# Attention and two MLPs on one core: eight steps' values scaled after the value matmul by sums from the tensor engine, with eight start-up banks, spread weight conversions and moved transfers

## The chip, the cores and the metric

One core of a Trainium2 chip runs the whole program in one launch. The metric is device time in microseconds (us), taken as the median of the runs. The profile is one execution of the same program, recorded by the hardware profiler. Five engines matter: TensorE (PE; weight loads are a row of their own, PEld), VectorE (DVE), ScalarE (ACT), GpSimd (POOL) and SyncE (SP), which issues most transfers.

## The reference

The inputs are 4 batches of 8 heads: 512 local and 32 global tokens of 64 features each. Local queries see the keys within 32 positions and all global keys; global queries see everything.

```python
def sm(s):
    s = s - np.max(s, axis=-1, keepdims=True)
    e = np.exp(s)
    return e / (np.sum(e, axis=-1, keepdims=True) + 1e-09)
...
s_l = np.concatenate([s_lg, s_ll], axis=-1)     # local rows: 32 global keys, then the masked local ones
a_l = sm(s_l)
out_l = np.matmul(a_l, np.concatenate([v_g, v_l], axis=2))
...
x = np.ascontiguousarray(attn_out.transpose(0, 2, 1, 3)).reshape(B * S, H * D)   # 2176 x 512
h = x @ w_in                       # first MLP, 512 -> 2048 -> 512
g = np.maximum(0.01 * h, h)
y = g @ w_out
h2 = y @ w2_in                     # second MLP, the same sizes
out = (h2 - np.tanh(h2)) @ w2_out
```

## The kernel before

**The attention.** The work on local queries is cut into 32 steps `pp`: two heads and a half (256 rows) of a batch each. `stage(s)` emits one slot of a software pipeline: transposes of keys and queries of step s+1 (`k_prep`, `q_prep`), scores of step s (`score`, tile `sps`), their softmax (`smax_a`, `smax_b`), the value matmuls of step s-2 (`av`, tile `avps`), scores of the global queries (`g_score`, `sgps`) and the transposes of the probabilities of step s-1 (`p_trans`, `ptps`). Every few stages a global query block is worked off (`g_smax`, `g_trans`, `g_av`).

In `smax_a` VectorE takes the minimum of the negated scores and ScalarE the exponential, with the row sum as a second output (`accum_out`). `smax_b` forms the reciprocal of four row sums per partition. For steps 0 to 7 GpSimd then multiplies the exponentials `e` by it (L453, two instructions of 128x512); for later steps VectorE does (L458). `p_trans` transposes the normalised `e` on TensorE and copies it out (`pt`; for steps 0 to 7 the second head's copy is VectorE's, L472). `av` multiplies by the values, and ScalarE (L500) and VectorE (L502) split the result into a high and a low part, `xh` and `xl`.

**The MLPs.** Every product is made of three float32r matmuls (high by high, low by high, high by low), so `mlp1_a` and `mlp1_b` issue 12 matmuls each per item. An item n is one 128-wide slice `f` of the hidden layer for one chunk `c` of tokens. Items 0 to 7 run beside stages 10 to 17, items 24 to 31 beside stages 18 to 21, items 32 to 63 beside the rest; items 8 to 23 have no attention beside them. The hidden tile `h` has one PSUM bank, so the next item's first matmul waits until ScalarE has read it (L206).

**Weights.** They come as 64-bit floats, two 32-bit words each. `convert_w` makes a 32-bit float of them with one ScalarE instruction (L128) and three of VectorE (L129, L133, L136); `split_w` makes the high and low parts (L142, L143). Four slices of `w_in` are converted in the start-up (stages 0 to 9), the others beside the items. `job()` converts slices of the other three matrices; each needs a raw tile `wraw`, of which there are two, fetched by SyncE in order. The table `job_at` says how many jobs an item has; the entry `early` adds one to some items.

**What sets the order.** TensorE runs in the order of the program text up to item 78. The other engines' order is set by a scheduler from the text's priorities and `issue_after`, which names an instruction that another must follow on its queue. Each engine runs its own list strictly in order. In the start-up seven PSUM banks are handed out in turn (`start_tags`), later three.

## Time and profile before

| what | value |
|---|---|
| median of 3 runs | 928.71 us (926.78 to 930.80) |
| the profiled execution | 928.65 us |
| its span, first to last instruction | 926.9 us |
| PE busy | 903.5 us (97%) |
| DVE busy | 628.0 us (68%) |
| ACT busy | 538.4 us (58%) |
| POOL busy | 38.8 us (4%) |
| mean granted TensorE clock | 0.998 of full speed |

The shares of the whole span say little here, because TensorE is busy nearly everywhere. What is open to a change is read from the stretches in which TensorE waits or runs small matmuls: the start-up (0 to about 64 us), and single waits later. Busy time of an engine in a stretch, the chain of waits through it and the single instructions on either side of a wait are the views to read.

### The profile page before, as it was taken

How to read it: one execution, taken by the hardware profiler on the slowest of the kernel's cores; microseconds unless marked ns; L12 is line 12 of the kernel's file. 1: busy time of each engine (PE TensorE's matmuls, PEld its weight loads, DVE VectorE, ACT ScalarE, POOL GpSimd, SP SyncE). 2: the span in 40 equal slices, each digit the busy share in tenths (PEclk: the TensorE clock that was granted, in tenths of full speed). 3: DMA queues.
4: the chain of work that ended last, by engine and by line, in shares of the span. 5: the costliest groups of instructions: out<-in, count | busy, mean ns of one | idle time of the engine just before them, and what ended most of it. 6: DMA issues, size and time to landing. Idle time of an engine off the chain costs nothing.

```text
span 926.9 us, 15545 instructions
## 1 busy us (share of the span) xinstructions
PE 903.5 (97%) x5468; PEld 766.3 (83%) x5468; DVE 628.0 (68%) x1373; ACT 538.4 (58%) x1245; POOL 38.8 (4%) x73
## 2 busy tenths in 40 slices
PE   7889999999899999999999999999999999999998
PEld 5667778887688999888889998888888888899897
DVE  3877867856545655643232459878888888888886
ACT  5888875444556666643233457555656655655664
POOL 4510000000000000000000000000000000000022
PEclk9999999999999999999999999999999999999999
DMA  8777798678866887767556662001000100010010
GB/s 191 189 195 196 220 282 265 199 220 273 278 187 180 246 227 235 221 211 226 174 187 199 222 199 92 1 1 59 22 1 24 46 1 0 1 47 1 1 35 24
DMA packets 146830, 129.22 MB, mean 139 GB/s; under 512 B 89536, under 2 KB 108992, under 8 KB 146752
## 3 DMA queue, kind: packets, MB, share of 16 engines
q1 hardware_dynamic: 144096, 127.57, 45.9%
q8 instruction: 43, 0.70, 0.3%
q10 hardware_dynamic: 2656, 0.66, 0.3%
q14 instruction: 35, 0.29, 0.1%
HBM read 101.45 MB, written 26.74 MB: 138 GB/s over the span
## 4 chain that ended last, share of the span: by engine, by line
PE 81%; DMA 6%; DVE 5%; ACT 5%; issue 1%; POOL 1%; SPq 0%; ACTq 0%; POOLq 0%; DVEq 0%
PE h L55 35%; PE o L55 20%; PE y L55 16%; DMA wf<-w2od 4%; PE sps L55 3%; PE ptps L469 2%; DMA wraw<-in_moe_w_out_dram 2%; ACT e L439 1%; PE avps L55 1%; DVE e L432 1%; PE gavps L55 1%; PE sgps L55 1%; PE kps L368 1%; ACT g L206 1%; DVE wf L136 1%
## 5 line engine op out<-in xcount | busy, mean ns | idle before, releaser
L55 PE MATMUL h<-xh,win 128*128 128x512 f32 (+2 forms) x1280 | 355.5, 361 | 1.6 <-ACT g L206 1.6
L55 PEld LDWEIGHTS h<-xh,win 128*128 128x128 f32 x1280 | 229.2, 188 | 34.3 <-ACT g L206 2.8
L55 PE MATMUL h<-xl,win 128*128 128x512 f32 (+2 forms) x640 | 229.0, 358 | 0.0
L55 PEld LDWEIGHTS h<-xl,win 128*128 128x128 f32 x640 | 120.5, 188 | 15.3
L55 PE MATMUL y<-gh,woh 128*128 128x512 f32 (+2 forms) x320 | 119.6, 374 | 0.0
L55 PE MATMUL y<-gh,wol 128*128 128x512 f32 (+2 forms) x320 | 114.9, 359 | 0.0
L55 PE MATMUL y<-gl,woh 128*128 128x512 f32 (+2 forms) x320 | 113.9, 359 | 0.0
L208 DVE TENSOR_TENSOR gl<-g,gh 128x512 fp32r<-128x512 f32 (+2 forms) x80 | 48.8, 611 | 90.4 <-ACT gh L207 86.3
L55 PE MATMUL o<-wo2l,gh 128*128 128x512 f32 x255 | 99.6, 391 | 0.0
L55 PE MATMUL o<-wo2h,gh 128*128 128x512 f32 x255 | 99.4, 390 | 0.0
L55 PE MATMUL o<-wo2h,gl 128*128 128x512 f32 x255 | 97.7, 390 | 0.0
L657 ACT ACTIVATE u<-h 128x512 f32<-128x512 f32 (+2 forms) x80 | 42.6, 533 | 93.1 <-PE h L55 86.2
L206 ACT ACTIVATE g<-h 128x512 f32<-128x512 f32 (+2 forms) x80 | 42.4, 530 | 73.4 <-PE h L55 73.2
L682 ACT ACTIVATE gh<-p 128x512 fp32r<-128x512 f32 (+2 forms) x80 | 45.5, 568 | 41.0 <-DVE p L666 41.0
L55 PEld LDWEIGHTS y<-gl,woh 128*128 128x128 f32 x320 | 60.5, 189 | 8.0
L55 PEld LDWEIGHTS y<-gh,woh 128*128 128x128 f32 x320 | 60.5, 189 | 7.6 <-issue 0.2
L55 PEld LDWEIGHTS y<-gh,wol 128*128 128x128 f32 x320 | 60.7, 190 | 6.5
L439 ACT ACTIVATE e<-e,st 128x224 f32<-128x224 f32 (+1 forms) x88 | 40.4, 460 | 29.1 <-DVE st L432 28.9
L663 ACT ACTIVATE u<-u,consts 128x512 f32<-128x512 f32 (+2 forms) x80 | 52.7, 659 | 6.9 <-DVE p L661 4.1
L683 DVE TENSOR_TENSOR gl<-p,gh 128x512 fp32r<-128x512 f32 (+1 forms) x64 | 41.9, 654 | 21.9 <-ACT gh L682 21.8
L55 PEld LDWEIGHTS o<-wo2h,gl 128*128 128x128 f32 x255 | 47.9, 188 | 10.2
L55 PEld LDWEIGHTS o<-wo2h,gh 128*128 128x128 f32 x255 | 48.0, 188 | 9.0
(111 smaller groups left out, 1401.1 us busy)
## 6 DMA issues: line engine op xcount, KB each, us to landing
wraw<-in_moe_w_out_dram SPq DMA_DIRECT2D x32, 512.0 KB, 4.6
woh<-wod SPq DMA_DIRECT2D x64, 256.0 KB, 3.9
wol<-wod SPq DMA_DIRECT2D x64, 256.0 KB, 3.4
inraw<-in_moe_w_in_dram SPq DMA_DIRECT2D x16, 512.0 KB, 5.9
wraw<-in_moe_w_in_dram SPq DMA_DIRECT2D x16, 512.0 KB, 5.3
vr<-in_v_l_dram SPq DMA_DIRECT2D x48, 96.0 KB, 3.8
kr<-in_k_l_dram SPq DMA_DIRECT2D x47, 96.0 KB, 3.2
wod<-woh SPq DMA_DIRECT2D x16, 256.0 KB, 4.2
```

The source lines that it names most:

```text
L55: nc.tensor.matmul(o, lhsT, rhs, start=start, stop=stop)
L136: nc.vector.scalar_tensor_tensor(out=w.bitcast(I32), in0=lw, scalar=29, in1=t, op0=ALU.logical_shift_right, op1=ALU.bitwise_or)
L206: nc.scalar.activation(g[:, :N], h[:, :N], AF.Prelu, alpha=0.01)
L208: anchor[0] = nc.vector.tensor_sub(gl[:, :N], g[:, :N], f32(gh)[:, :N])
L368: nc.tensor.transpose(ps[:, c : c + n], kr[:n, t].rearrange("p h d -> p (h d)"), ident[:n, :n])
L432: nc.vector.tensor_tensor_reduce(out=e[:, h, j, s0 : s0 + n], in0=ps[h][:, j * 256 : j * 256 + n], in1=mask[:, a, j, :n], op0=ALU.add, op1 ...
L439: last_exp[0] = nc.scalar.activation(e[:, h, j, s0 : s0 + n], x, AF.Exp, bias=st[:, k : k + 1], scale=-1.0, accum_out=st[:, 4 + k : 5 + k],)
L469: nc.tensor.transpose(ps[:, at : at + n], e[:n, h, j, c0 : c0 + 128], ident[:n, :n])
L657: nc.scalar.activation(u, h, AF.Square)
L663: nc.scalar.activation(u, u, AF.Square, bias=tc_a2)
L682: nc.scalar.activation(gh[:, :N], p, AF.Copy)
L683: eng["pool" if i == order2[-1] else "dve"].tensor_sub(gl[:, :N], p, f32(gh)[:, :N])
```

## The change

Steps 0 to 7 (`late`) no longer normalise `e`. The exponential has no second output, and `smax_b` does nothing for them. In `av`, besides the eight matmuls by the values, eight more multiply the same transposed `e` by a constant block of ones (`ones`, 64 columns of `consts`), so that the other half of the same bank holds each query's row sum, repeated over the 64 rows of its head. VectorE adds 1e-9 (L510), takes the reciprocal of 128x256 (L511) and multiplies (L512); the copy and the difference that split the result read that product.

The start-up hands out eight banks: `h` joins the seven. The four conversions of the start-up are cut in parts (`convert_parts`) that are emitted between the operations of stages 3, 5, 7 and 9 in place of whole ones after stages 2, 4, 6 and 8. The second jobs of items 22 and 23 go: `early` has 8 entries, 17 among them, and not 9; the later jobs come every 9.5 and not every 9.8 units. The two loads of partial sums in `y_part` must follow the newest fetch of output weights on SyncE's list. In the last chunk of the first MLP, `w2_place` runs behind the newest instructions of the item.

```diff
+    ones = consts[:, 32:96]
...
-    def norm(pp):
-        return "pool" if pp < 8 else "dve"
+    def late(pp):
+        return pp < 8
...
-                    accum_out=st[:, 4 + k : 5 + k],
+                    **({} if late(pp) else {"accum_out": st[:, 4 + k : 5 + k]}),
...
+        if late(pp):
+            return
         nc.vector.tensor_scalar_add(st[:, 4:8], st[:, 4:8], 1.0e-9)
         nc.vector.reciprocal(st[:, 8:12], st[:, 4:8])
-        if norm(pp) == "pool":
-            r = st[:, 8:12].rearrange("p (h j) -> p h j", h=2)
-            for h in range(2):
-                nc.gpsimd.tensor_mul(e[:, h], e[:, h], r[:, h].unsqueeze(2).to_broadcast([128, 2, 256]))
-            return
...
         for j in range(2):
-            for c, (_, n, t, lo, hi) in enumerate(chunks[pp // NP % 2][j]):
-                for h in range(2):
-                    r = slice(64 * h, 64 * h + 64)
-                    q = slice(j * 128 + lo, j * 128 + hi)
+            for k in range(2 if late(pp) else 1):
+                for c, (_, n, t, lo, hi) in enumerate(chunks[pp // NP % 2][j]):
                     at = pt_at[2 * j + c][0]
-                    mm(ps[r, q], v[:n, t, h], pt[h][:n, at + lo : at + hi], c == 0, c == 1)
-        nc.scalar.activation(dh, ps[:, :HALF], AF.Copy)
+                    for h in range(2):
+                        r = slice(64 * h, 64 * h + 64)
+                        q = slice(k * HALF + j * 128 + lo, k * HALF + j * 128 + hi)
+                        mm(ps[r, q], ones[:n] if k else v[:n, t, h], pt[h][:n, at + lo : at + hi], c == 0, c == 1)
+        x = ps[:, :HALF]
+        if late(pp):
+            x = mlp.tile([128, HALF], F32, tag="gl", name="xs", bufs=3)
+            nc.vector.tensor_scalar_add(x, ps[:, HALF:], 1.0e-9)
+            nc.vector.reciprocal(x, x)
+            nc.vector.tensor_mul(x, ps[:, :HALF], x)
+        nc.scalar.activation(dh, x, AF.Copy)
         av_n.append(pp)
-        last_av[0] = nc.vector.tensor_sub(dl, ps[:, :HALF], f32(dh))
+        last_av[0] = nc.vector.tensor_sub(dl, x, f32(dh))
...
-        nc.sync.dma_start(out=f32(x)[:, :, 256:512], in_=yp_dram[:, :, 256 * k : 256 * k + 256])
+        with tc.issue_after(last_fetch[0].ins):
+            nc.sync.dma_start(out=f32(x)[:, :, 256:512], in_=yp_dram[:, :, 256 * k : 256 * k + 256])
...
-    start_tags = ["att0", "att1", "att2", "y0", "y1", "y2", "y3"]
+    start_tags = ["att0", "att1", "att2", "y0", "y1", "y2", "y3", "h"]
...
-        early = n in (11, 12, 13, 15, 16, 18, 20, 22, 23)
+        early = n in (11, 12, 13, 15, 16, 17, 18, 20)
...
-        job_at[n] = int(out_f) + int(early) + int(due / 9.8)
-        due %= 9.8
+        job_at[n] = int(out_f) + int(early) + int(due / 9.5)
+        due %= 9.5
...
-            for op in stage(pp):
+            parts = in_parts() if pp >= 3 and pp % 2 else []
+            for k, op in enumerate(stage(pp)):
                 op()
+                if parts and k != 1:
+                    behind(parts.pop(0))
...
-            if pp >= 2 and pp % 2 == 0:
-                in_job()
...
-                    w2_place(kind, f, t)
+                    behind(lambda: w2_place(kind, f, t))
```

On TensorE, the value matmuls of one start-up step (`vr` are values, `consts` the ones), as a piece of the difference:

```order
 L55 MATMUL avps<-pt,vr 64x128 x2
 L55 MATMUL avps<-pt,vr 64x64 x2
+L55 MATMUL avps<-pt,consts 64x128 x2
+L55 MATMUL avps<-pt,consts 64x64 x2
 L55 MATMUL avps<-pt,vr 64x128 x2
 L55 MATMUL avps<-pt,vr 64x96 x2
+L55 MATMUL avps<-pt,consts 64x128 x2
+L55 MATMUL avps<-pt,consts 64x96 x2
```

Eight matmuls by the ones have come between the eight by the values; the profile counts each of them as two.

On VectorE, stage 4 of the start-up before: `sps_514` are the scores of step 4, `avps_530` the product of step 2, `st` the row sums, `inraw1` a raw slice of `w_in`:

```order
L502 TENSOR_TENSOR xl512_69<-avps_530,xh512_67 128x256
L472 COPY pt_562<-ptps_557 128x480
L448 TENSOR_SCALAR st_523<-st_523 128x4
L129 TENSOR_SCALAR wt_564<-wf_565 128x512
L449 RECIPROCAL st_523<-st_523 128x4
L133 SCALAR_TENSOR_TENSOR wt_564<-inraw1_339,wt_564 128x512
L136 SCALAR_TENSOR_TENSOR wf_565<-inraw1_339,wt_564 128x512
L426 TENSOR_REDUCE st_593<-sps_584 128x2
```

The same stage after the change, where `avps_539` is the product of step 2 and `xs_556` the scaled one:

```order
L136 SCALAR_TENSOR_TENSOR wt_430<-inraw0_217,wt_430 128x512
L510 TENSOR_SCALAR xs_556<-avps_539 128x256
L141 SCALAR_TENSOR_TENSOR wf_418<-inraw0_217,wt_430 128x512
L511 RECIPROCAL xs_556<-xs_556 128x256
L478 COPY pt_579<-ptps_574 128x480
L149 TENSOR_TENSOR win0_498<-wf_418,win0_498 128x512
L512 TENSOR_TENSOR xs_556<-avps_539,xs_556 128x256
L435 TENSOR_REDUCE st_605<-sps_596 128x2
L435 TENSOR_REDUCE st_605<-sps_597 128x2
L515 TENSOR_TENSOR xl512_69<-xs_556,xh512_67 128x256
```

The add and the reciprocal come ahead of the copy of the transposed exponentials, and the minimum of the next step stands behind the product that needs the reciprocal. The conversion of the slice is spread between them.

On ScalarE, from the activation of item 22 on, before (`wf` and `w2f` are conversions that need a `wraw`; `kt` and `qt` belong to stage 18, beside item 24):

```order
L206 ACTIVATE g_2857<-h_2844 128x512
L207 ACTIVATE gh_2858<-g_2857 128x512
L128 ACTIVATE wf_2879<-wraw_2834 128x512
L142 ACTIVATE woh_2884<-wf_2879 128x512
L128 ACTIVATE w2f_2890<-wraw_2842 128x512
L206 ACTIVATE g_2915<-h_2902 128x512
L207 ACTIVATE gh_2916<-g_2915 128x512
L128 ACTIVATE wf_2937<-wraw_2888 128x512
L370 ACTIVATE kt_2963<-kps_2959 128x352
L381 ACTIVATE qt_2968<-qps_2965 128x256
```

The same place after the change:

```order
L212 ACTIVATE g_2923<-h_2910 128x512
L213 ACTIVATE gh_2924<-g_2923 128x512
L129 ACTIVATE wf_2943<-wraw_2863 128x512
L148 ACTIVATE woh_2949<-wf_2943 128x512
L212 ACTIVATE g_2972<-h_2959 128x512
L213 ACTIVATE gh_2973<-g_2972 128x512
L129 ACTIVATE wf_2992<-wraw_2908 128x512
L148 ACTIVATE woh_2998<-wf_2992 128x512
L377 ACTIVATE kt_3019<-kps_3015 128x352
L388 ACTIVATE qt_3024<-qps_3021 128x256
```

Before, three conversions stand between the activation of item 22 and the keys and queries of stage 18, two of them ahead of the activation of item 23; after, there are two, one for each item.

## Rows read from the trace of the kernel before

**Rows 1.** Page, busy per engine, and TensorE's slices of 23 us in tenths:

```profile
PE 903.5 (97%) x5468; PEld 766.3 (83%) x5468; DVE 628.0 (68%) x1373; ACT 538.4 (58%) x1245; POOL 38.8 (4%) x73
...
PE   7889999999899999999999999999999999999998
```

**Rows 2.** Busy time by stretch: start-up stages 2 to 9, then ten-microsecond windows:

```profile
core 0: us, PE busy (x) PEld busy (x) DVE busy (x) ACT busy (x) POOL busy (x), PEclk, DMA share, GB/s
17.22:63.94 46.72, 40.89 (x442) 31.05 (x440) 36.01 (x88) 38.01 (x130) 17.17 (x18) 1.00 0.76 188
...
220.00:230.00 10.00, 9.32 (x42) 7.35 (x41) 6.98 (x12) 4.07 (x7) 0.00 (x0) 1.00 0.85 274
230.00:240.00 10.00, 7.15 (x50) 5.44 (x48) 5.77 (x19) 5.65 (x17) 0.00 (x0) 0.85 1.02 350
...
530.00:540.00 10.00, 9.67 (x55) 9.13 (x53) 3.88 (x6) 4.93 (x10) 0.00 (x0) 1.00 0.75 239
540.00:550.00 10.00, 9.53 (x55) 9.53 (x56) 4.92 (x8) 5.36 (x11) 0.00 (x0) 1.00 0.78 255
```

**Rows 3.** Chain of waits, start-up: start, length, what:

```profile
17.22 1.33 PE sps L55 x10
...
27.52 1.49 PE sps L55 x10
...
45.38 0.87 PE avps L55 x16
...
63.94 0.95 PE sps L55 x8
```

**Rows 4.** Single instructions: start, length, idle before and releaser; stages 1, 2 and 5:

```profile
15.06 0.63 PE L469 MATMUL ptps<-ident,e 128*128 128x128 f32 x4 [0.46 <-POOL e L453]
...
16.06 0.64 PE L469 MATMUL ptps<-ident,e 128*128 128x128 f32 x4 [0.36 <-POOL e L453]
...
16.53 0.47 PE L368 MATMUL kps<-ident,kr 128*128 128x128 f32 x3
...
31.88 0.54 PE L55 MATMUL sps<-mask,ident_b 128*128 128x448 bf16 x2
```

**Rows 5.** Groups by line in stages 2 to 9: count, busy, mean, idle before:

```profile
L136 DVE SCALAR_TENSOR_TENSOR wf<-inraw,wt 128x512 int32<-128x512 int32 x5 | 5.6, 1122 | 0.1
...
L449 DVE RECIPROCAL st<-st 128x4 f32<-128x4 f32 x9 | 1.6, 175 | 0.2
...
L448 DVE TENSOR_SCALAR st<-st 128x4 f32<-128x4 f32 x9 | 1.5, 163 | 0.9 <-ACT e L439 0.8
...
L439 ACT ACTIVATION_READ_ACCUMULATOR e<-sps,st 128x1 f32 x32 | 6.6, 205 | 0.0
```

**Rows 6.** One line's instructions over the run: shortest, median, longest in ns:

```profile
L582 DVE RECIPROCAL gst<-gst x8: 155/162/166, 41.0 to 405.2; 128x1 f32<-128x1 f32 x8
...
L449 DVE RECIPROCAL st<-st x32: 170/178/179, 13.6 to 402.1; 128x4 f32<-128x4 f32 x32
...
L502 DVE TENSOR_TENSOR xl<-avps,xh x32: 412/425/427, 21.5 to 439.7; 128x256 fp32r<-128x256 f32 x32
...
L133 DVE SCALAR_TENSOR_TENSOR wt<-inraw,wt x16: 681/692/693, 22.3 to 178.4; 128x512 int32<-128x512 int32 x16
```

**Rows 7.** Single instructions around item 24, with idle before and releaser:

```profile
228.10 1.24 SPq L224 DMA_DIRECT2D xl<-yp  x1
...
228.35 0.73 PE L55 MATMUL h<-xh,win 128*128 128x512 f32 x2 [0.68 <-ACT g L206]
...
231.59 0.67 ACT L128 ACTIVATE wf<-wraw 128x512 f32<-128x512 f32 x1 [2.63 <-DMA wraw<-in_moe_w_out_dram]
...
232.17 0.44 ACT L370 ACTIVATE kt<-kps 128x352 f32<-128x352 f32 x1
...
237.35 0.80 PE L55 MATMUL sgps<-kt,qgd 128*64 128x128 f32 x6 [2.85 <-DVE st L432]
```

**Rows 8.** Waits in stages 2 to 9: total, times, longest:

```profile
DVE xl L502 <- ACT xh L500: 3.5, 5, 1.0
```

More of the change, by code (lines that the diff above doesn't have):

```diff
@@ L114, in load_w, with convert_parts, first, second @@
         return raw
-    nw = [0]
-    def convert_w(raw, w=None):
+    def convert_parts(raw, w=None):
         hw, lw = raw[:, :, 1], raw[:, :, 0]
-        t = mlp.tile([128, DM], I32, tag="wt", name="wt", bufs=1)
         if w is None:
             w = mlp.tile([128, DM], F32, tag="wf", name="wf", bufs=2)
-        nw[0] += 1
-        nc.scalar.activation(w, hw.bitcast(F32), AF.Copy, scale=REBIAS)
-        nc.vector.tensor_scalar(
-            out=t, in0=w.bitcast(I32), scalar1=3, scalar2=0x7FFFFFFF,
-            op0=ALU.logical_shift_left, op1=ALU.bitwise_and,
-        )
-        nc.vector.scalar_tensor_tensor(
-            out=t, in0=hw, scalar=-0x80000000, in1=t, op0=ALU.bitwise_and, op1=ALU.bitwise_or
-        )
-        nc.vector.scalar_tensor_tensor(
-            out=w.bitcast(I32), in0=lw, scalar=29, in1=t, op0=ALU.logical_shift_right, op1=ALU.bitwise_or
-        )
-        return w
+        t = []
+        def first():
+            t.append(mlp.tile([128, DM], I32, tag="wt", name="wt", bufs=1))
+            nc.scalar.activation(w, hw.bitcast(F32), AF.Copy, scale=REBIAS)
+            nc.vector.tensor_scalar(
+                out=t[0], in0=w.bitcast(I32), scalar1=3, scalar2=0x7FFFFFFF,
+                op0=ALU.logical_shift_left, op1=ALU.bitwise_and,
+            )
+        def second():
+            nc.vector.scalar_tensor_tensor(
+                out=t[0], in0=hw, scalar=-0x80000000, in1=t[0], op0=ALU.bitwise_and, op1=ALU.bitwise_or
+            )
+        def third():
+            nc.vector.scalar_tensor_tensor(
+                out=w.bitcast(I32), in0=lw, scalar=29, in1=t[0], op0=ALU.logical_shift_right, op1=ALU.bitwise_or
+            )
+        return w, [first, second, third]
     def split_w(w, hi, lo, lo_engine):
@@ L168 @@
     last_exp = [None]
-    last_kq = [None]
+    last_kq, last_fetch = [None], [None]
     av_n = []
@@ L733, in in_load, with behind, converted, in_parts @@
                 in_raw.append((f, load_w("in", w1_in, f, place)))
-    def converted(raw, w=None):
-        with ExitStack() as behind:
+    def behind(part):
+        with ExitStack() as stack:
             for x in (last_av, last_exp, anchor, anchor_s):
                 if x[0] is not None:
-                    behind.enter_context(tc.issue_after(x[0].ins))
-            return convert_w(raw, w)
-    def in_job():
-        if in_raw:
-            f, raw = in_raw.pop(0)
-            w = converted(raw)
+                    stack.enter_context(tc.issue_after(x[0].ins))
+            part()
+    def converted(raw, w=None):
+        w, parts = convert_parts(raw, w)
+        for part in parts:
+            behind(part)
+        return w
+    def in_parts():
+        if not in_raw:
+            return []
+        f, raw = in_raw.pop(0)
+        w, parts = convert_parts(raw)
+        def split():
             t = win_tile(f)
             split_w(w, t[:, 0], t[:, 1], nc.vector)
+        return parts + [split]
+    def in_job():
+        *parts, split = in_parts() or [lambda: None]
+        for part in parts:
+            behind(part)
+        split()
     jobs, raws = [], []
@@ L916 @@
         nc.vector.memset(tc_a2, T_A2)
+        nc.vector.memset(ones, 1.0)
         build_masks()
```

2 lines of the change are left out of this document (1 added, 1 removed).

## The prediction

> **What bounds the kernel now.** I began with the page: TensorE is busy for 903.5 of 926.9 us, and its slices fall below nine tenths only in the first three (to about 70 us) and the last [rows 1]. The reader is to see that the gain to be had is small and sits in few places, and that shares of the whole span don't price this change. So I went on by stretch. In stages 2 to 9 of the start-up, 46.72 us, TensorE is busy 40.89, ScalarE 38.01, VectorE 36.01 and GpSimd 17.17 [rows 2]: no engine is full, but three are near it, and whichever gets more work soon sets the length. The chain of waits gives the ends of that stretch, the scores of stage 2 at 17.22 and of stage 10 at 63.94, that is 5.84 us a stage [rows 3]. The shortest stage, 27.52 to 31.88, takes 4.36 [rows 3, 4]. What makes most stages longer than that is the string minimum, exponential, sum, GpSimd's product, transpose, copy, with everybody's queue in order.
>
> The other place is 220 to 240 us. TensorE is idle there for 0.68 + 2.85 = 3.53 us, and the clock granted over 230 to 240 averages 0.85 [rows 2]. Single instructions tell why [rows 7]: SyncE puts the two loads of partial sums out (the second takes 1.24 us to issue at 228.10), the next conversion of ScalarE waits 2.63 us for its raw tile until 231.59, behind it stand the keys of stage 18 (232.17) and the activation of item 24, and in the end TensorE's score matmul at 237.35 waits 2.85 us for VectorE's minimum.
>
> **The change part by part.** The profiled execution took 928.65 us, 1.75 more than its span and 0.06 less than the median, so the sum is made against 928.65 and read as a median.
>
> *GpSimd's product goes.* In stage 1 the transposes of step 0 wait 0.46 and 0.36 us for it and start 1.00 us apart, where four of them need 0.47 without a wait (16.06 to the keys at 16.53) [rows 4]. TensorE was free for them at 15.06 - 0.46 = 14.60, so the keys come at 14.60 + 2 x 0.47 = 15.54: 1.0 us, before there is any value matmul to pay for. With GpSimd's product goes what looks like its collision with VectorE: L136 has a mean of 1.12 us over five in this stretch [rows 5], against 0.69 for its twin L133 [rows 6], so 5 x 0.43 = 2.2 us of VectorE. ScalarE loses 32 sum reads, 6.6 us [rows 5], and falls to about 31 us busy: it can't be the bound then.
>
> *Matmuls by the ones come.* They have the shapes of the value matmuls, and 16 of those (as the profile counts) take 0.87 us [rows 3]. Eight steps: 7.0 us of TensorE. The shortest stage would be 5.23, eight of them 41.8; the other end is 40.89 + 6.96 = 47.9, if nothing of the busy time is a wait. So TensorE alone allows between 41.8 and 47.9 us.
>
> *Three VectorE instructions of 128x256 come, in place of two of 128x4.* Add and product each read PSUM and are like L502, 0.42 us [rows 6]. A reciprocal of that size is nowhere in the trace. From below it costs what the other instructions of 256 columns cost, 0.42. From above: two sizes are there, 162 ns for one column and 178 for four [rows 6], so 5.3 ns a column, and 0.162 + 255 x 5.3 ns = 1.52 us. I take 1.52, since the row is the same operation; both ends are kept for the range. VectorE's sum for stages 2 to 9: 36.0 busy, less seven pairs of 0.175 + 0.163 = 2.4 [rows 5], less the 2.2 of the collision, plus 8 x (0.42 + 1.52 + 0.42) = 18.9. That is 50.3 us, more than the stretch has now and more than TensorE's 47.9. VectorE becomes the bound of the start-up, and I take the stretch at 50.3, which is 3.6 longer. What stands behind the reciprocal on VectorE's list is the copy of the transposed exponentials, which the next value matmuls need, and the next step's minimum: nothing can slip past it.
>
> [...]
>
> *Eighth bank, spread conversions.* Four conversions stay in the start-up, and their instructions are in the 36.0 already, so they cost nothing new. With eight allocations a stage and eight banks, the next value matmuls land in the bank that the product has just left. That closes a loop: 2 x 0.87 of matmuls, 0.42, 1.52, the copy, 0.42, about 4.8 us without a conversion and near 6.2 with two parts of one in between (0.69 each). It agrees with 50.3 / 8 = 6.3, so I add nothing. If the parts should hide, the loop is shorter; if they pile up, the last rival holds.
>
> *Jobs and transfers around item 24.* One conversion fewer stands ahead of the keys of stage 18, and the two loads of partial sums go out some 30 transfers later. The 3.53 us of idle time and the slow clock (15% of 10 us, 1.5) go: 5.0. Late next are the double jobs of items 17, 18 and 20, three within four items; TensorE isn't stopped there now (its slices from 162 to 209 us are full [rows 1]), so I keep 0.4 back: 4.6 less. The loads themselves have until the sums are needed in the last items of that chunk, and are hidden. The bounds are 0 and 5.0.
>
> *Weights of the second MLP.* Behind the item's own activations they can no longer stand in their way. TensorE is idle 0.33 + 0.47 = 0.80 us at 530 to 550 [rows 2]; I take 0.3 of it. Bounds 0.8 less, and as much more. The jobs every 9.5 units fall where TensorE is full and ScalarE is not: nothing.
>
> Sum: 928.65 - 1.0 + 3.6 - 4.6 - 0.3 = 926.35, so **926.4**, 0.25% less: two real effects that nearly cancel.
>
> **The rivals.**
> *The reciprocal is as cheap as an add* (0.42). Then VectorE needs 50.3 - 8 x 1.10 = 41.5 and TensorE is the bound; I take 46.5 of its 41.8 to 47.9, since its list has waits besides. 928.65 - 1.0 - 0.2 - 4.6 - 0.3 = 922.5. For it: 16 ns between two tiny sizes is weak evidence for a slope. Against it: 5.3 ns a column is not the 1.04 ns that rows of 256 and 512 columns give (0.692 - 0.425 over 256 [rows 6]).
> [...]
> *The stall doesn't go but moves* to items 17 to 20, seven jobs in four items with two raw tiles: the 4.6 come back, 931.0. The change of the transfers would then not do what it says. Against it: neither the loads of partial sums nor a stage of attention stands there.
> *VectorE's difference waits for ScalarE's copy.* The difference L515 stands ahead of the next add and the next conversion parts, and needs a copy that ScalarE does after keys and queries. Before, that wait is at most 1.0 us and 3.5 over the stretch [rows 8], and VectorE had slack. On a full VectorE each is lost; at 1.0 a step, 8 x 1.0 more: 934.4, slower. It decides from about 0.9 us a step on.
>
> **How the numbers follow.** A measurement of this kernel can't tell less than about 0.5% (4.6 us) from no change, so faster means under 924.0 and slower over 933.3. Forecast 0.45, its own range 923 to 930; cheap reciprocal 0.20; eight passes 0.12; the stall moves 0.12; the difference waits 0.11. Faster: 0.17 of the cheap case, 0.14 of the forecast's, 0.02 of the rest, 0.33. Slower: 0.07 of the last rival, 0.06 of the eight passes, 0.03 of the others, 0.16. The remainder, 0.51, is within 0.5%. The range 920.5 to 933.5 takes in the cheap case and most of the slow ones, and leaves out the rest of the last rival and combinations of good luck.
>
> **What would show it.** In the profile after: the reciprocal at 1.5 us with VectorE busy over nine tenths of stages 2 to 9, and those stages 49 to 52 us long; the transposes of step 0 starting by 14.7; L136's twin at 0.69; TensorE's idle time of 220 to 240 under 0.5 us and the clock at 1.0 there. I am wrong if the reciprocal is under 0.8 or over 2 us, if stages 2 to 9 are shorter than 45 or longer than 55 us, or if TensorE waits at items 17 to 24.

## The result and the profile after

The changed kernel takes **933.41 us** (median of 7 runs, 931.88 to 934.91) against 928.71 (926.40 to 930.89) for the kernel before: a ratio of 1.0053, 95% interval 1.0037 to 1.0068. It is slower by 4.7 us, where 2.3 us less had been forecast: the sign is wrong. The profiled execution took 934.21 us with a span of 932.4, 5.5 us longer than before's 926.9, and it is the one that is taken apart here.

The page of the changed kernel, engines' busy time and TensorE's slices, answers to [rows 1]:

```profile
PE 908.1 (97%) x5596; PEld 772.1 (83%) x5596; DVE 639.0 (69%) x1382; ACT 538.0 (58%) x1213; POOL 20.1 (2%) x57
...
PE   7889999999999999999999999999999999999998
```

At this scale nothing is to be seen; the difference sits in a few stretches. Its busy time by stretch (the columns are those of [rows 2]; the first row is stages 2 to 9):

```profile
15.35:67.08 51.73, 44.81 (x571) 36.97 (x568) 45.65 (x86) 37.58 (x106) 0.60 (x4) 1.00 0.80 202
...
67.08:76.24 9.16, 7.55 (x68) 6.21 (x68) 8.17 (x30) 5.53 (x19) 0.00 (x0) 0.81 0.57 129
...
210.00:220.00 10.00, 8.82 (x39) 6.99 (x38) 7.84 (x13) 4.82 (x9) 0.00 (x0) 1.00 0.72 246
220.00:230.00 10.00, 10.00 (x44) 7.98 (x43) 6.16 (x10) 5.29 (x9) 0.00 (x0) 1.00 0.85 254
230.00:240.00 10.00, 10.00 (x51) 8.08 (x52) 5.66 (x10) 4.62 (x9) 0.00 (x0) 1.00 0.84 258
...
550.00:560.00 10.00, 8.36 (x48) 7.95 (x47) 5.61 (x10) 5.81 (x11) 0.00 (x0) 1.00 0.52 180
```

Stages 2 to 9 take 51.73 us in place of 46.72, with VectorE busy 45.65 of them, 88%. The stall of 220 to 240 us is gone (TensorE 20.0 of 20, clock 1.00). New are a slow clock in the stretch from the scores of stage 10 to item 0 (67.08 to 76.24, 0.81), an idle 1.18 us at 210 to 220 and 1.64 us at 550 to 560.

To see where the time goes along the run, I subtract the start of item k's activation before (L206) from the same one after (L212). All later tables do this; "end" is the difference of the spans.

| us later than before | item 0 | 17 | 22 | 25 | 70 | end |
|---|---|---|---|---|---|---|
| changed kernel | 6.2 | 6.2 | 8.4 | 3.0 | 3.4 | 5.5 |

So: 6.2 lost in the start-up, 2.2 more at the double jobs, 5.4 won at item 24 (3.2 net of both), 2.1 lost at the end of the first MLP. The scores of stage 2 begin 1.7 us earlier than before, those of stage 10 3.2 later: 4.9 are lost in stages 2 to 9, and 3.0 more between the scores of stage 10 and item 0, which the prediction did not have at all.

Groups of VectorE in stages 2 to 9 (line, operation, names and shapes, count, busy, mean in ns, idle before):

```profile
L511 DVE RECIPROCAL xs<-xs 128x256 f32<-128x256 f32 x8 | 14.0, 1750 | 0.2
...
L515 DVE TENSOR_TENSOR xl<-xs,xh 128x256 fp32r<-128x256 f32 x8 | 3.3, 418 | 1.7 <-ACT xh L513 1.7
L510 DVE TENSOR_SCALAR xs<-avps 128x256 f32<-128x256 f32 x8 | 3.3, 417 | 1.0 <-PE avps L55 0.9
L512 DVE TENSOR_TENSOR xs<-avps,xs 128x256 f32<-128x256 f32 x8 | 3.3, 412 | 0.0
...
L141 DVE SCALAR_TENSOR_TENSOR wf<-inraw,wt 128x512 int32<-128x512 int32 x3 | 2.0, 678 | 0.0
```

The reciprocal takes 1.75 us; add and product are 0.42 and 0.41, as taken. L141 here does what L136 did before, at 1.12 us on the mean [rows 5]; now it is at 0.68. In the trace before, three of those five took 1.41 us, each while GpSimd's product ran, and the others 0.69:

```profile
33.07 2.84 POOL L453 TENSOR_TENSOR e<-e,st 128x512 f32<-128x512 f32 x2 [1.46 <-DVE st L449]
33.60 1.41 DVE L136 SCALAR_TENSOR_TENSOR wf<-inraw,wt 128x512 int32<-128x512 int32 x1
```

So the collision was real, and it is gone. VectorE hardly waits in front of any of the groups above.

What TensorE does there, single instructions (start, length, engine and line, operation, in brackets the idle time before and its releaser), and VectorE's list ahead of the one at 45.35:

```profile
33.31 0.56 PE L55 MATMUL avps<-pt,vr 128*64 128x128 f32 x8 [1.32 <-DVE xs L512]
...
45.35 0.40 PE L533 MATMUL qgps<-ident,qgr 32*128 32x32 f32 x4 [1.80 <-issue]
...
52.62 0.36 PE L55 MATMUL sps<-mask,ident_b 128*128 128x448 bf16 x1 [1.11 <-DVE xs L512]
...
59.89 0.41 PE L384 MATMUL qps<-ident,qr 128*128 128x128 f32 x2 [1.51 <-issue]
...
71.39 0.78 PE L55 MATMUL gavps<-pg,vn 96*64 96x32 f32 x20 [1.37 <-DVE st L441]
```

```profile
42.07 1.74 DVE L511 RECIPROCAL xs<-xs 128x256 f32<-128x256 f32 x1
43.73 0.59 DVE L478 COPY pt<-ptps 128x480 f32<-128x480 f32 x1
44.25 0.67 DVE L149 TENSOR_TENSOR win<-wf,win 128x512 fp32r<-128x512 f32 x1
44.84 0.41 DVE L512 TENSOR_TENSOR xs<-avps,xs 128x256 f32<-128x256 f32 x1
```

The profile names the product L512 as the end of the waits at 33.31 and 52.62. For those at 45.35 and 59.89 it names no releaser, but each ends where a product L512 does (44.84 + 0.41, 59.37 + 0.41). At all four places the operation gets, by rotation of the eight banks, one that holds values not yet scaled, and the product stands behind the reciprocal, and here behind a copy and a part of a conversion too. Together they are 5.74 of the 6.92 us that TensorE is idle in stages 2 to 9.

At 71.39 TensorE waits for a minimum of stage 10 that stands late on VectorE's list: VectorE is busy for 8.17 of the 9.16 us from the scores of stage 10 to item 0. Seven of its 30 instructions there are parts of the last two weight conversions; before, two stood there. TensorE's clock in the stretch is 0.81 on the mean. The same stretch before, with nearly the same matmuls:

```profile
63.94:70.05 6.11, 5.42 (x67) 4.48 (x68) 4.37 (x19) 4.45 (x16) 0.00 (x0) 1.00 0.85 236
```

The end of the first MLP, ScalarE in the changed kernel (a first block) and before (a second):

```profile
554.43 0.63 ACT L148 ACTIVATE wo2h<-wf 128x512 fp32r<-128x512 f32 x1 [1.55 <-DMA wf<-w2od]
556.36 0.63 ACT L148 ACTIVATE win<-wf 128x512 fp32r<-128x512 f32 x1 [1.30 <-DMA wf<-w2id]
556.90 0.58 ACT L670 ACTIVATE u<-h 128x512 f32<-128x512 f32 x1
```

```profile
547.63 0.64 ACT L142 ACTIVATE wo2h<-wf 128x512 fp32r<-128x512 f32 x1 [1.16 <-DMA wf<-w2od]
549.02 0.60 ACT L657 ACTIVATE u<-h 128x512 f32<-128x512 f32 x1 [0.76 <-DVE wo2l L143]
549.52 0.49 ACT L206 ACTIVATE g<-h 128x384 f32<-128x384 f32 x1
550.85 0.63 ACT L142 ACTIVATE win<-wf 128x512 fp32r<-128x512 f32 x1 [0.84 <-DMA wf<-w2id]
```

Before, the split of `win` stood behind the item's activation; now both splits stand ahead of the next one, each waiting for its transfer. The first activation of the second MLP is 7.9 us later than before, and TensorE waits for what hangs on it: 1.64 us at 559.34, 1.01 at 572.32.

### The profile page after: what moved, and what is told of

It is laid out like the page before. It is cut to its first block, busy times and chain, and to the rows that moved or that the text cites. A ratio compares the mean times of both kernels' runs of the same rounds, so it can differ in the third digit from the quotient of the medians.

```text
span 932.4 us, 15714 instructions
## 1 busy us (share of the span) xinstructions
PE 908.1 (97%) x5596; PEld 772.1 (83%) x5596; DVE 639.0 (69%) x1382; ACT 538.0 (58%) x1213; POOL 20.1 (2%) x57
## 4 chain that ended last, share of the span: by engine, by line
PE 83%; DMA 6%; DVE 6%; ACT 3%; issue 1%; SPq 0%; DVEq 0%; ACTq 0%
PE h L55 36%; PE o L55 20%; PE y L55 16%; PE sps L55 3%; PE ptps L475 2%; DMA wf<-w2od 2%; PE avps L55 2%; DMA wf<-w2id 2%; DVE e L441 1%; PE gavps L55 1%; DMA wraw<-in_moe_w_out_dram 1%; PE sgps L55 1%; PE kps L375 1%; PE qps L384 1%; DMA kr<-in_k_l_dram 1%
## 5 line engine op out<-in xcount | busy, mean ns | idle before, releaser
L212 ACT ACTIVATE g<-h 128x512 f32<-128x512 f32 (+2 forms) x80 | 42.5, 531 | 88.5 <-PE h L55 88.4
```

The lines of the kernel that those rows point to most:

```text
L212: nc.scalar.activation(g[:, :N], h[:, :N], AF.Prelu, alpha=0.01)
```

## The experiments

Theories on the start-up: **full VectorE** (the reciprocals take VectorE's time, and what TensorE needs stands behind them) against **held bank** (the bank is kept through add, reciprocal and product). Each run was timed beside the kernel before, whose medians on the chip lay between 928.5 and 929.5.

| run | median us | ratio to before, 95% | item 17 | 22 | 25 | 70 | end |
|---|---|---|---|---|---|---|---|
| changed kernel | 933.41 | 1.0053 (1.0037–1.0068) | 6.2 | 8.4 | 3.0 | 3.4 | 5.5 |
| e1_place_free | 933.00 | 1.0047 (1.0030–1.0065) | 8.2 | 9.1 | 4.1 | 4.8 | 4.7 |
| e2_no17 | 933.53 | 1.0063 (1.0041–1.0086) | 8.6 | 8.4 | 3.5 | 3.5 | 4.8 |
| e3_old_table | 936.78 | 1.0092 (1.0065–1.0119) | 8.3 | 9.0 | 4.6 | 4.6 | 6.9 |
| e4_no_recip | 928.52 | 0.9992 (0.9971–1.0012) | 3.7 | 4.1 | -1.0 | -0.7 | 1.5 |
| e5_bank_free | 936.44 | 1.0072 (1.0050–1.0095) | 10.4 | 12.5 | 6.9 | 7.3 | 9.2 |
| e6_no_add | 930.76 | 1.0024 (1.0011–1.0037) | 4.3 | 5.3 | -0.1 | 0.3 | 1.5 |
| e7_pool | 927.59 | 0.9977 (0.9962–0.9992) | 0.9 | 1.2 | -3.8 | -3.4 | -2.8 |
| e8_all_mended | 926.27 | 0.9967 (0.9951–0.9983) | 2.7 | 2.5 | -2.4 | -1.8 | -2.4 |
| e9_pool_mended | 924.40 | 0.9950 (0.9931–0.9970) | 0.9 | 0.7 | -4.2 | -3.8 | -4.3 |
| e10_pool_product | 931.32 | 1.0026 (1.0012–1.0040) | 7.0 | 6.8 | 2.0 | 2.1 | 2.4 |
| e11_pool_whole | 923.14 | 0.9937 (0.9916–0.9957) | -0.7 | -0.9 | -5.8 | -5.8 | -5.0 |
| e12_seven_banks | 935.94 | 1.0084 (1.0058–1.0110) | 9.2 | 9.8 | 4.5 | 4.8 | 7.2 |
| e13_idle_recip | 932.26 | 1.0034 (1.0018–1.0049) | 4.1 | 5.4 | 0.4 | 0.8 | 2.8 |
| e14_ones_whole | 935.39 | 1.0079 (1.0054–1.0104) | 9.1 | 9.4 | 4.3 | 4.6 | 5.7 |
| e15_idle_placed | 939.28 | 1.0108 (1.0090–1.0127) | 12.5 | 13.7 | 8.7 | 9.1 | 10.5 |
| e16_product_alone | 927.69 | 0.9981 (0.9967–0.9996) | 4.0 | 3.8 | -1.0 | -0.7 | -0.9 |

One caution for the table: e1 to e3 have the start-up of the changed kernel, but stand at 8.2 to 8.6 at item 17 in place of 6.2. Their profiled runs have a granted clock of 0.68 to 0.73 over 45 to 50 us, with TensorE idle for 1.1 to 1.5 of the 5 us before; that of the changed kernel has 1.00, with 1.8 idle. Start-ups of two profiles compare to about 2 us, differences inside one profile and medians better.

**e1_place_free**

```
-                    behind(lambda: w2_place(kind, f, t))
+                    w2_place(kind, f, t)
```


> The changed kernel, only the splitting of the second MLP's weights in the last chunk is free again, as before. Theory (in the changed kernel two weight splits stand ahead of each item's activation on ScalarE, each waiting for its transfer, where before one stood ahead and one behind; so the first activations of the second MLP come late): the last 2.4 us of the loss, between the last chunk of the first MLP and the second MLP, go: 931.0, ratio to before about 1.0025. Rival (the loss there is only a matter of when the shifted program meets its transfers): 933.4, within 0.8 us.

In the profile it loses nothing from item 70 to the end (4.8 to 4.7), where the changed kernel loses 2.1, and TensorE's idle time there is gone. The median doesn't show it: 933.00 is 0.4 us below the changed kernel's, within the rival's range, and the two intervals are too wide to tell 2 us. Over all profiles the picture is clear: with the weights held behind the activations, item 70 to the end costs 0.6 to 2.4 us (eleven profiles, mean 1.7), and without that -0.6 to 0.8 (six, mean 0.0). The row of e1 for 550 to 560:

```profile
550.00:560.00 10.00, 9.84 (x56) 9.39 (x55) 6.17 (x11) 6.89 (x14) 0.00 (x0) 1.00 0.56 174
```

**e2_no17**

```
-        early = n in (11, 12, 13, 15, 16, 17, 18, 20)
+        early = n in (11, 12, 13, 15, 16, 18, 20)
...
-        job_at[n] = int(out_f) + int(early) + int(due / 9.5)
-        due %= 9.5
+        job_at[n] = int(out_f) + int(early) + int(due / 9.1)
+        due %= 9.1
```


> The changed kernel without the second job of item 17 (later jobs every 9.1 units, so that all are placed). Theory (double jobs of items 17 and 18 in a row use both raw tiles, and ScalarE waits for the third with the activation behind it): the delay of activations at items 18 to 22, 2.8 us at item 21 or 22, is gone, and item 25 stands about 0.2 us later than before in place of 2.96: 930.6. Rival (two raw tiles are too few for any double job there, 18 and 20 too): delay at items 18 to 22 stays over 1.5 us, 932.5 to 933.4.

Nothing is lost at items 18 to 22 any more (8.6 to 8.4), and from item 17 to 25 it wins 5.0. The six runs without the job at 17 all win 5.0 to 5.1; those with the new table and the job win 3.2 to 4.8. In the changed kernel that job holds an activation up behind a raw tile; first ScalarE's conversion, then TensorE's wait for the activation:

```profile
209.55 0.66 ACT L129 ACTIVATE wf<-wraw 128x512 f32<-128x512 f32 x1 [2.53 <-DMA wraw<-in_moe_w_out_dram]
```

```profile
213.32 0.73 PE L55 MATMUL h<-xh,win 128*128 128x512 f32 x2 [1.18 <-ACT g L212]
```

The median, 933.53 where 930.6 was expected, doesn't show the gain; its interval overlaps that of the changed kernel.

**e3_old_table**

```
-        early = n in (11, 12, 13, 15, 16, 17, 18, 20)
+        early = n in (11, 12, 13, 15, 16, 18, 20, 22, 23)
...
-        job_at[n] = int(out_f) + int(early) + int(due / 9.5)
-        due %= 9.5
+        job_at[n] = int(out_f) + int(early) + int(due / 9.8)
+        due %= 9.8
```


> The changed kernel with the old table of jobs (second jobs at items 22 and 23, none at 17, every 9.8 units); the two loads of partial sums stay moved. Theory (the jobs made the stall at item 24, the loads only worsened it): TensorE again idles 1.5 to 3.5 us at 230 to 245 us, item 25 stands 4 to 6 us later than before: 934.5 to 936.6. Rival (the two loads made it): no idle time there, item 25 about 0.5 us later than before at 6.2 - 5.0 = 1.2: 931.5.

The median, 936.78, lies just over the theory's 934.5 to 936.6 and far from the rival's 931.5, and TensorE still waits 1.23 us for a minimum at 243.28, so the table has a part in the stall. But in the profile the moved loads alone, with the old table, win 3.7 from item 17 to 25, and e2's table 1.3 more (5.0): the larger part was the loads of partial sums. Neither expectation had it so.

**e4_no_recip** (the reciprocal is replaced by an add of a constant, so the values aren't normalised)

```
-            nc.vector.reciprocal(x, x)
+            nc.vector.tensor_scalar_add(x, x, 1.0)
```


> The changed kernel with an add of a constant in place of the 128x256 reciprocal, so the eight steps' values are scaled by the wrong factor; everything else is as in the changed kernel. Theory (VectorE is the bound of the start-up through the reciprocal's 1.75 us, and its backlog delays stage 10): stages 2 to 9 take 46 to 48 us (51.7 in the changed kernel), the 3.0 us lost from stage 10 to the first activation go: 925 to 927. Rival (the matmuls by the ones, 7 us of TensorE, are the bound): stages 2 to 9 keep at least 50 us: 931 to 933.

0.9992 against 1.0053: the eight reciprocals, against an add in their place, are worth 5.7 us of the median, more than the whole loss. With them gone VectorE is busy 39.40 of 48.67 us and TensorE 46.18:

```profile
15.83:64.50 48.67, 46.18 (x570) 38.57 (x567) 39.40 (x96) 36.99 (x108) 0.61 (x4) 0.96 0.74 183
```

TensorE is then nearly full (95%) and VectorE is not. The stretch is 1.95 us longer than before's, about what a clock of 0.96 costs in it. The 3.0 us from the scores of stage 10 to item 0, which the theory had going too, did not go. That stretch in e4 and, below it, in e7_pool, which has no such reciprocals either (see there):

```profile
64.50:73.27 8.77, 7.33 (x67) 5.96 (x67) 5.00 (x20) 4.93 (x17) 0.00 (x0) 0.81 0.77 200
```

```profile
63.11:70.44 7.33, 5.86 (x67) 4.73 (x67) 5.32 (x20) 4.81 (x16) 0.00 (x0) 1.00 0.88 235
```

Against 6.11 before, e7 is 1.2 us longer at a full clock, and e4 2.7 with a clock of 0.81, although VectorE is busy for only 5 us in either. So the loss there isn't the reciprocals' alone.

**e5_bank_free**

```
+            vs = mlp.tile([128, HALF], F32, tag="gh", name="vs", bufs=3)
+            nc.scalar.activation(vs, ps[:, :HALF], AF.Copy)
...
-            nc.vector.tensor_mul(x, ps[:, :HALF], x)
+            nc.vector.tensor_mul(x, vs, x)
```


> The changed kernel, with the value half of each of the first eight avps banks copied to SBUF by ScalarE right behind its matmuls (one copy of 128x256, about 0.41 us, eight in all); the product reads that copy, so the bank comes free after the add and the copy and not after add, reciprocal and product. VectorE's work stays as it is. Theory 'held bank': the two waits of TensorE before the transposes qgps (1.8 us) and qps (1.5 us), which end with a product, go, and the start-up is some 3.3 us shorter: 930.5 to 931.5. Rival 'full VectorE': the eight reciprocals and their neighbours are the bound themselves, the waits only change their name: 933 to 934.5.

Freeing the bank early won nothing: 936.44, no faster than the changed kernel. The waits at the product went (all four), and a longer one came, for a scaling that stands behind a conversion part and a reciprocal on VectorE:

```profile
44.13 0.68 DVE L141 SCALAR_TENSOR_TENSOR wf<-inraw,wt 128x512 int32<-128x512 int32 x1
44.73 1.74 DVE L513 RECIPROCAL xs<-xs 128x256 f32<-128x256 f32 x1
46.39 0.40 DVE L598 TENSOR_SCALAR sg<-sg,gst 128x544 f32<-128x544 f32 x1
```

```profile
46.94 0.85 PE L608 MATMUL gtps<-ident,sg 128*112 128x128 f32 x4 [4.36 <-DVE sg L598]
```

TensorE is idle for 7.0 us of stages 2 to 9, as much as in the changed kernel. A granted clock of 0.72 over 45 to 50 us and 0.60 over 50 to 55, behind that wait, costs 3.4 us more.

**e6_no_add**

```
-            nc.vector.tensor_scalar_add(x, ps[:, HALF:], 1.0e-9)
-            nc.vector.reciprocal(x, x)
+            nc.vector.reciprocal(x, ps[:, HALF:])
```


> The changed kernel without the eight adds of 1e-9 to the sums (each at least 1, since the largest exponential of a row is 1); the reciprocal reads the bank itself. VectorE has 8 x 0.41 = 3.3 us less to do, each bank is held 0.41 us less. Theory 'full VectorE': the start-up is 3.3 us shorter, 930.5 to 931. Rival 'held bank': only the two waits become 0.4 us shorter, 0.8 us in all: 933.

1.0024 against 1.0053: 2.7 us for 3.3 us less of VectorE, as the full VectorE has it. Each result is ready 0.41 us sooner as well, so this run doesn't part VectorE's time from the later results.

**e7_pool**

```
     def late(pp):
-        return pp < 8
+        return False
...
+        if pp < 8:
+            r = st[:, 8:12].rearrange("p (h j) -> p h j", h=2)
+            for h in range(2):
+                nc.gpsimd.tensor_mul(e[:, h], e[:, h], r[:, h].unsqueeze(2).to_broadcast([128, 2, 256]))
+            return
```


> The changed kernel with the probabilities of the first eight steps made again by GpSimd, as before, and no matmuls by the ones; eight banks, spread conversions, moved transfers and the new table stay. If the loss is in the new normalisation (by either theory of it), the start-up takes what it took before or less, the gain at item 24 stays (3.2 us), the late loss too (2 to 2.5 us): 927 to 929.5. If the other edits made the loss in the start-up (spread conversions above all), it stays: 932 to 934.

0.9977: with GpSimd's product kept, the rest of the change is a gain. The new normalisation alone costs 0.76%, about 7 us. The third part of a conversion (L141) takes 0.69 us here too, with GpSimd's product in place: the spread parts don't fall in GpSimd's time, so the collision would have gone without the new normalisation. In e11_pool_whole, with GpSimd's product and whole conversions, the mean is 1.04.

**e8_all_mended** (e1, e2, e5 and e6 in one)

```
-            nc.vector.tensor_scalar_add(x, ps[:, HALF:], 1.0e-9)
-            nc.vector.reciprocal(x, x)
-            nc.vector.tensor_mul(x, ps[:, :HALF], x)
+            vs = mlp.tile([128, HALF], F32, tag="gh", name="vs", bufs=3)
+            nc.scalar.activation(vs, ps[:, :HALF], AF.Copy)
+            nc.vector.reciprocal(x, ps[:, HALF:])
+            nc.vector.tensor_mul(x, vs, x)
...
-                    behind(lambda: w2_place(kind, f, t))
+                    w2_place(kind, f, t)
```


> The changed kernel with four edits: no add, the value half copied away by ScalarE, the second MLP's weights split where they were before, no double job at 17 (the due time's divisor 9.1 in place of 9.5). If the losses add up (held bank or full VectorE 3.3 us, late splits about 1 us, job 17 about 0.6 us): 934.1 - 4.9 = 929.2, and 926 if the held bank and VectorE's work each count for themselves. If a next bound stands close behind, as the wait of gavps in the run without the reciprocals: 930 to 931.

926.27: with the matmuls by the ones the kernel can beat the one before, by 0.33%. That is the 926 expected if the held bank and VectorE's work each count; which of the four edits brought how much can't be read from it.

**e9_pool_mended** (e1, e2 and e7 in one) and **e11_pool_whole** (the same, with `in_job()` behind every even step in place of the spread parts)

```
-            parts = in_parts() if pp >= 3 and pp % 2 else []
+            parts = []
...
+            if pp >= 2 and pp % 2 == 0:
+                in_job()
```


> The changed kernel with GpSimd's product of before in the first eight steps, the second MLP's weights split where they were before, and no double job at 17 (divisor 9.1). The run with GpSimd's product alone stood at 927.6 with its start-up 0.9 us longer than before's, its stall at item 24 4.7 us shorter and a late loss of 1.0 us. If these parts add: 927.6 - 1.0 - 0.4 = 926.2; not under 925 and not over 927.5.

> The kernel of the run e9_pool_mended with the conversions of the first MLP's weights in one piece behind every even step, as before, in place of spread over the odd steps. If the spread conversions are worth anything by themselves, it is slower than that one, by the 0 to 1.5 us that a whole conversion (2.4 us of VectorE) can hold up a step; if they only move the same work, the two are within 0.5 us.

e9 is below its range, e11 the fastest of all: 923.14 us, 0.63% under before, where slower or the same had been expected. The intervals of the two overlap, so a price of the spread conversions isn't shown.

**e14_ones_whole** (the last diff, on the changed kernel)

> The changed kernel with the conversions in one piece behind every even step, as before. With GpSimd's product the whole conversions were 1.3 us faster than the spread ones. If that is their own price, 932 to 933 here. If the spread conversions are what lets VectorE take the reciprocals at all, a whole conversion (2.4 us) beside a reciprocal (1.75 us) in one step makes it 935 or more.

1.0079, 2.4 us above the changed kernel's ratio, with intervals that still overlap. It points to the spread being of use only where the reciprocals are.

**e10_pool_product** (on e8_all_mended)

```
-            nc.vector.tensor_mul(x, vs, x)
+            nc.gpsimd.tensor_mul(x, vs, x)
...
-        last_av[0] = nc.vector.tensor_sub(dl, x, f32(dh))
+        last_av[0] = (nc.gpsimd if late(pp) else nc.vector).tensor_sub(dl, x, f32(dh))
```


> The mended kernel (no add, values copied away by ScalarE, late splits and job 17 undone: 926.3) with the product by the reciprocals and the subtraction of the low part on GpSimd in the first eight steps, where it has 128x256 x 16 to do; VectorE keeps of each step's normalisation only the reciprocal and has 8 x 0.83 = 6.6 us less. Theory 'full VectorE': its start-up loses the 2.7 us that it still takes over before's: 923.5 to 924.5. Rival, that the chain of a step (reciprocal, product, copy, subtraction) and not VectorE's load sets the pace, and GpSimd is slower at it: 926.5 to 930.

Slower by 5 us than e8, against the theory's number and beyond the rival's 930 too. The edit did two things: the conversions are tied to that subtraction, and when it left VectorE's list they moved. VectorE now stands idle for ScalarE's half of a conversion, with a reciprocal queued behind it:

```profile
32.50 0.43 DVE L130 TENSOR_SCALAR wt<-wf 128x512 int32<-128x512 int32 x1 [1.82 <-ACT wf L129]
32.84 1.75 DVE L512 RECIPROCAL xs<-avps 128x256 f32<-128x256 f32 x1
```

Three of its five third parts of a conversion run beside GpSimd's work again and take 1.09 to 1.21 us, so the run says little about either theory.

**e16_product_alone** (on e8_all_mended; the subtraction stays on VectorE)

```
-            nc.vector.tensor_mul(x, vs, x)
+            nc.gpsimd.tensor_mul(x, vs, x)
```

> The run e8_all_mended (926.3) with the product by the reciprocals alone on GpSimd; the subtraction stays on VectorE, and with it the place of the conversions that are tied to it, which e10_pool_product had moved. VectorE has 8 x 0.41 = 3.3 us less. Theory 'VectorE's time': 923.5 to 925.5. Rival 'chain of the result': GpSimd took 0.86 us for the product against 0.41, the result is 0.45 us later in each step: 926.5 to 930.

0.9981 against e8's 0.9967: 3.3 us less of VectorE won nothing. GpSimd takes 0.73 us for the product, so each result is later, and the median is that of the rival. The profile is less plain: stages 2 to 9 take 48.78 us against e8's 49.06, and the loss is from the scores of stage 10 to item 0, 9.24 us against 6.71, with a clock of 0.82 against 1.00. That the reciprocal also costs as one link of a string (sum, reciprocal, product, copy) fits this but isn't shown.

**e12_seven_banks**

```
-    start_tags = ["att0", "att1", "att2", "y0", "y1", "y2", "y3", "h"]
+    start_tags = ["att0", "att1", "att2", "y0", "y1", "y2", "y3"]
```


> The changed kernel with seven banks in the rotation of the start-up, as before, in place of eight. Theory 'full VectorE': the eighth bank is worth nothing, 933.5 to 934.5. Rival 'held banks': with one bank less the reuse comes sooner, TensorE's two waits of 1.5 to 1.8 us grow and others come, 936 or more.

1.0084: by the ratios the eighth bank is worth some 3 us here, though the two intervals overlap. With seven, TensorE waits for the product at six places (two that the profile leaves unnamed end with it), 8.4 us in all; three of them:

```profile
28.13 0.36 PE L55 MATMUL sps<-mask,ident_b 128*128 128x448 bf16 x1 [0.97 <-DVE xs L512]
...
35.17 0.36 PE L55 MATMUL sps<-mask,ident_b 128*128 128x448 bf16 x1 [1.96 <-DVE xs L512]
...
41.81 0.36 PE L55 MATMUL sps<-mask,ident_b 128*128 128x448 bf16 x1 [1.57 <-DVE xs L512]
```

The held bank is thus real. Eight banks make the waits fewer, four and 5.74 us, and don't cover it.

**e13_idle_recip** and **e15_idle_placed** (on e7_pool: reciprocals for nobody; the line with `issue_after` is in e15 alone)

```
+            idle = mlp.tile([128, HALF], F32, tag="gl", name="idle", bufs=3)
+            with tc.issue_after(last_av[0].ins):
+                nc.vector.reciprocal(idle.rearrange("p (a n) -> p a n", a=4), ones.unsqueeze(1).to_broadcast([128, 4, 64]))
```


> The run e7_pool (GpSimd's product, 927.6) with eight reciprocals of 128x256 on VectorE added, where the changed kernel has them, of a constant and for nobody: no bank is held for them, no result waits for them, only VectorE is 1.75 us busy, eight times (14.0 us). Theory 'VectorE's time': with VectorE at 33.9 us of the 47.5 from 16.5 to 64 it has 13.6 us free, but each reciprocal stands ahead of the next minimum or copy that TensorE waits for: 4 us or more longer, 931.5 to 934. Rival 'chain of the result': what costs is that bank, product, copy and subtraction wait for the reciprocal; then this one is within 1 us of 927.6.

> The run e7_pool (GpSimd's product, 927.6) with eight idle reciprocals of 128x256 on VectorE, each held behind the subtraction of its step, so that they stand spread over stages 2 to 9 (in e13_idle_recip the scheduler put all eight ahead of stage 2, where they cost 5 us as one block). Nobody waits for their results and no bank is held. Theory 'VectorE's time': what they push back is what TensorE needs next, 931.5 to 934. Rival 'chain of the result': within 1 us of 927.6, and the cost in the changed kernel lies in what waits for the reciprocal.

In e13 the scheduler put all eight ahead of stage 2, so it measured a delay of the start; in e15 they are spread (first and last start, in us, behind the durations; e13 first, then e15):

```profile
L515 DVE RECIPROCAL idle<-consts x8: 1694/1694/1753, 1.0 to 12.4; 128x256 f32<-128x256 f32 x8
```

```profile
L524 DVE RECIPROCAL idle<-consts x8: 1735/1742/1745, 21.7 to 73.3; 128x256 f32<-128x256 f32 x8
```

e15 is 1.3% slower than e7, 12 us for 13.9 us of reciprocals that hold no bank and that nobody waits for, and far over the 934 of its theory. The profile tells why: about half is the clock. It is 0.62 to 0.70 in four windows, in or ahead of which TensorE pauses: 2.24 us up to 26.15, 0.82 up to 45.09, 1.95 up to 47.67 and 2.11 up to 60.68. These four windows cost 1.7, 1.5, 1.9 and 1.7 us, 6.8 in all, of the 13.3 by which the profiles' spans differ (e7's clock is full over its start-up):

```profile
25.00:30.00 5.00, 3.59 (x17) 2.48 (x17) 4.93 (x8) 3.48 (x11) 3.58 (x5) 0.66 0.89 225
...
45.00:50.00 5.00, 2.96 (x15) 2.44 (x16) 2.61 (x7) 2.36 (x7) 2.07 (x3) 0.70 0.51 117
50.00:55.00 5.00, 5.00 (x49) 3.70 (x51) 1.16 (x2) 2.04 (x9) 0.00 (x0) 0.62 0.45 126
...
60.00:65.00 5.00, 4.32 (x50) 4.26 (x51) 4.04 (x8) 2.67 (x12) 2.59 (x3) 0.66 0.73 165
```

The other half are waits of TensorE for what stands behind the reciprocals, above all GpSimd's product (5.6 us over 16 to 68 us, 3.2 in e7), which the changed kernel doesn't have:

```profile
PE ptps L480 <- POOL e L464: 5.6, 7, 2.2
PE avps L55 <- DVE gst L604: 2.1, 1, 2.1
```

VectorE's time alone, with the clock that follows the waits, is thus enough for a loss of this size, without anyone waiting for the results. That it is so in the changed kernel too is inferred from this and from e4 and e6, not shown.

## Why the prediction was wrong

The forecast was a small gain, and the kernel became slower. That 933.41 is still just inside the stated range is luck: the range went so far up for the rivals' sake, and neither the loss behind stage 10 nor that at the late weights was foreseen at its size.

By its own steps, predicted and measured (profile after against before):

| term | predicted | measured |
|---|---|---|
| GpSimd's product gone, to stage 2 | -1.0 | -1.7 |
| stages 2 to 9 | +3.6 | +4.9 |
| stage 10 to item 0 | not in the sum | +3.0 |
| double jobs and item 24 | -4.6 | -3.2 |
| late weights | -0.3 | +2.1 |
| between | 0 | +0.4 |
| sum | -2.3 | +5.5 |

*GpSimd's product.* Right, and somewhat small: the eight transposes of step 0 now start at 13.93 and run without a wait.

```profile
13.93 1.05 PE L475 MATMUL ptps<-ident,e 128*128 128x128 f32 x8
14.82 0.47 PE L375 MATMUL kps<-ident,kr 128*128 128x128 f32 x3
```

*Stages 2 to 9.* The mechanism was in the main the forecast one: the reciprocal on VectorE sets the pace. Without it the kernel is 5.7 us faster (e4), and 5.74 us of TensorE's waits end at the product behind it. The size was off in two ways that nearly cancel. VectorE's busy time is 45.65 us, 4.6 less than the 50.3 of the sum, although the reciprocal took 1.75 us and not 1.52 (8 x 0.23 = 1.8 more; the slope from 162 to 178 ns [rows 6] was the right evidence and a seventh short). "Four conversions stay in the start-up, and their instructions are in the 36.0 already" overlooked that the change moves some out of the stretch: five conversion instructions and four normalisations, 4.5 us, stand behind its end now. The sum also added whole durations to a busy time in which neighbours overlap (43.73 + 0.59 is past 44.25 in the list above). And the stretch is 6.1 us longer than that busy time, since VectorE waits too, which the sum left out. The prediction's test, over nine tenths busy, failed at 88%.

ScalarE didn't fall to about 31 us either but stays at 37.58, for a like reason: the sum reads that went had overlapped other instructions. TensorE waits for it only 0.9 us in the stretch, so this decided nothing.

*The step that failed first* is the end of that stretch. The sum stopped at the scores of stage 10 and put nothing behind them. But from there to item 0 TensorE is idle for 9.16 - 7.55 = 1.61 us, before for 0.69, and a clock of 0.81 costs 19% of 9.16, 1.7 us. These are 2.6 of the 3.0. What makes the idle time is open: VectorE is nearly full there, with the conversion parts that came from the stretch before, but without the reciprocals TensorE is idle for nearly as long (1.44 in e4, 1.47 in e7), in part for a transfer of values. All three have the spread conversions; e11_pool_whole, which hasn't, takes 5.7 us for this stretch.

*"The next value matmuls land in the bank that the product has just left ... so I add nothing."* At 33.31 the value matmuls did wait for it, 1.32 us, and at three more places other operations met a held bank. Still these 5.74 us are no further term: they are how TensorE waits for the full VectorE. With the bank freed early (e5) TensorE is idle for as long, for something else behind a reciprocal. Adding nothing for it stands.

*Item 24.* The stall went, as forecast, and 5.0 is its worth (six runs). What came back is 1.8 us at the double jobs of items 17 and 18 in this profile, where 0.4 had been kept back for what was named as late next: undersized, and the prediction's own sign of being wrong, a wait of TensorE at items 17 to 24, came true (1.18 us at 213.32). e2 shows job 17 to be the cause.

*The second step that failed* is the late weights. "Behind the item's own activations they can no longer stand in their way" is wrong: behind the latest activation means ahead of the next item's, and there each split waits for its transfer. The sign was wrong and 2.1 lies outside the bound of 0.8 more (e1).

*The rivals.* The cheap reciprocal fell at 1.75 us. No run shows the eight passes that the chances name; the runs show 1.75 us for 256 columns, 4.2 times the 0.417 of the add. The moved stall came true in part. VectorE's wait for ScalarE's copy is 1.7 us over eight steps, less than before's 3.5 [rows 8]: that rival gave nearly the measured time (934.4) by a mechanism that is not there, which is luck.

What stays open: how the 5.7 us of the reciprocals divide between VectorE's time and the later results (e6, e10 and e16 change both), what makes the idle time from stage 10 to item 0, and whether the spread conversions gain or lose.

## What to carry to other kernels

Work added to one of several busy engines can cost nearly its full time before that engine shows as full: 13.9 us of reciprocals that nobody used cost 12, half as waits and half as the slower clock (6.8 us in the profile), with VectorE busy for 35.76 of the 47.50 us from 16.5 to 64 us, 75% (e15). Look past the end of the stretch too, and see which instructions the change pushes there: here 3.0 us were lost behind the last stage that the sum had. Add durations to a busy time only after looking how far neighbours overlap. Where an engine takes its list in order, "behind x" means "ahead of what follows x" (here the activation at 556.90, behind two splits that waited 1.55 and 1.30 us for their transfers): look at what that is, and whether the moved instruction waits for a transfer.

## What was not expected of the hardware

- A reciprocal of 128x256 takes 1.75 us on VectorE, and the same from PSUM (1.756 in e16): about 6.2 ns a column from the 162 ns of one column [rows 6].
- The granted clock was lower in some windows with a short pause of TensorE just before or in them: over 70 to 75 us it was 0.71 in the changed kernel (1.37 us idle up to 71.39), and 0.66 in e4 (0.79 up to 68.66), e6 (0.69 up to 69.66) and e16 (1.37 up to 69.45). Eight transposes took 1.80 us there (73.54, changed kernel), 1.05 at a clock of 1.00 (64.16). The start-up of the changed kernel showed 0.68 to 0.73 at 45 to 50 us in e1 to e3, and 1.00 in its own profile, with 1.80 us idle up to 45.35: so it is no fixed cost.
- VectorE's third part of a conversion took 1.41 us where it ran beside GpSimd's product (three of five) and 0.69 elsewhere (before); in e7, which has both but not at the same time, it took 0.69.
- GpSimd's product of 128x256 took 0.73 us on the mean in e16, and 0.86 in e10, where the subtractions are GpSimd's too.
